# Gated attention and feed-forward decode on one core: sixteen small loads behind the second item's keys

## The chip, the cores and the metric

The kernel runs on one core of a Trainium2 chip. The metric is the time of one execution on the device in microseconds. TensorE is called PE here, VectorE DVE, ScalarE ACT, GpSimd POOL and SyncE SP; SP issues every DMA of this kernel, and 16 DMA engines carry them out.

## The reference

Two tokens (batch B = 2, one position each, width D = 640) go through attention with 32 heads over a cache of 4096 keys and values of 128 numbers per head, and through a feed-forward layer of width 1728. A gate mixes the two results. All is float32.

```python
def reference(A_x, A_k_cache, A_v_cache, A_wq, A_wo, B_x, B_w1, B_w2, gate_w):
    x = A_x
    g = sigmoid((x * gate_w).sum(-1, keepdims=True))
    q = (x @ A_wq).reshape(B, 1, 32, 128).transpose(0, 2, 1, 3)
    p = softmax(einsum("bhqd,bhkd->bhqk", q, A_k_cache) * 128 ** -0.5)
    o = einsum("bhqk,bhkd->bhqd", p, A_v_cache)
    a = o.transpose(0, 2, 1, 3).reshape(B, 1, 4096) @ A_wo
    b = einsum("bsf,fd->bsd", silu(einsum("bsd,df->bsf", x, B_w1)), B_w2)
    return g * a + (1 - g) * b
```

The keys and the values are 134 MB each; wq and wo are 10.5 MB each, w1 and w2 4.4 MB each.

## The kernel before

The attention is cut into 16 items: eight groups of four heads, times two batches. An item has one load of keys and one of values, each 128 partitions of 64 KB (8.4 MB). SBUF holds three such slabs: "v" for values, "a" and "b" for the keys of even and odd items. Since "a" and "b" alternate, the keys of item i + 2 can be loaded when the scores of item i are made, and the values of item i + 1 when PE has used those of item i.

Per item, POOL and DVE multiply the keys by the query, each a part of the slab (lines 670 and 676); DVE sums the products into scores (line 686) and finds the peak (lines 694 to 704); ACT makes the exponentials (line 715); PE multiplies them by the values (line 766); DVE and PE then bring the result into the columns of `oP` (lines 788 to 837). Before the items stand the query weights wq (line 608) and the feed-forward layer: w1 is loaded into slab "a", DVE forms the hidden row (lines 443 and 446), spreads and turns it into the buffer `turned` (line 499), and ACT and DVE make `seq` from it (lines 500 to 512). Nothing reads `turned` after line 512. After the items, PE multiplies `oP` by wo (lines 556 and 586), and one store of 5 KB writes the output.

The order on each engine is the order in which the program writes its operations. A small planner (`Flow.plan`, line 75) goes through all operations and gives each one the waits on semaphores that its reads and writes need, and leaves out those that are already implied. `Flow.dma` (line 67) records a DMA; all of them are on SP, so they have line 69 in the profile. SP works through its list in order: an instruction that waits holds up all that stand behind it. A DMA has a semaphore of its own unless one is given by `signal`, which it raises by 16 when all of it has landed.

SP's list around the change: w1, x, gate, w2, wq, a store of zeros, then the keys of the first item (`load_k(0)`, line 470), the values of the first item and the keys of the second (`load_v(0)` and `load_k(1)`, lines 656 and 657), and then, from the loop at line 853, `load_k(i + 2)` and `load_v(i)` in turn. In the texts below k0, k1, k2 are the keys of the first, second and third item, and v0 the values of the first.

Of the kernel before, what the change touches and what calls it, by code (L numbers as in the profile page):

```python
# [158 lines left out]
def gated_decode(nc, x, kc, vc, wq, wo, w1, w2, gate, out):  # L159
# [31 lines left out]
    f = Flow(nc)  # L191
    V, S_, T_, G_ = nc.vector, nc.scalar, nc.tensor, nc.gpsimd

    def sb(name, shape, align=32):
        return nc.alloc_sbuf_tensor(name, shape, F32, align_bytes=align)[tuple([slice(None)] * len(shape))]
# [9 lines left out]
    def part(n, *ks):  # L205
        return [f"{n}.{k}" for k in (ks or range(8))]
# [21 lines left out]
    turned = sb("turned", [P, FR * 32])  # L228
# [17 lines left out]
    oT = ps_m[:64, 256:512].rearrange("p (n r) -> p n r", r=32)  # L246
    early, acc = ps_acc[:, :W2], ps_0[:, :W]

    h_q, h_e, h_v, h_o = (f.sem(n) for n in ("next_q", "weights", "values", "rows"))


# [9 lines left out]
    def kslab(i):  # L261
        return "a" if i % 2 == 0 else "b"
# [4 lines left out]
    def run_of(flat, i):  # L267
        hq, b = items[i]
        return flat[b, hq].rearrange("(p c) -> p c", p=P)

    def load_k(i):
        n = kslab(i)
        f.dma("SP", slab[n], run_of(kflat, i), writes=part(n))
# [3 lines left out]
    def load_v(i):  # L277
        src = run_of(vflat, i)
        if i < N - 1:
            v_load[i] = f.dma("SP", slab["v"], src, writes=part("v"), signal=h_v if i < LOOPED else None)  # L280
            return
        f.dma("SP", slab["a"], src, writes=part("a"))
# [112 lines left out]
    for e in range(2):  # L395
        ends, at = join[:, e, ::HB], 64 + HB * (1 - e)
# [40 lines left out]
    for b in range(B):  # L437
        for j in range(J):
            at = xt[:, j, HB * b : HB * b + 1]
# [177 lines left out]
    def mm_query(i):  # L617
        return T_.matmul(  # L618
            ps_q[:, :DH],
            spread,  # L620
            qall.rearrange("p h b d -> p (h b) d")[:, i, :],
            start=True,
            stop=True,
        )

    def query(i, by=(), loop=None):
        u, b = items[i][0] // HALF, items[i][1]
        fn = (lambda: mm_query(i)) if loop is None else (lambda it: mm_query(it + i))
        f.op(
            "PE",  # L630
            fn,
            reads=["spread", f"qall{u}{b}"],
            writes=["ps_q"],
            by=by,
            loop=loop,
            lower=[(h_q, 1)],
        )

    def copy_q(i):
        f.op("ACT", lambda: S_.copy(qsb, ps_q[:, :DH]), reads=["ps_q"], writes=["qsb"])  # L640
# [14 lines left out]

    load_v(0)
    load_k(1)
    query(0)
    copy_q(0)

# [4 lines left out]
    def products(i):  # L665
        k = slab[kslab(i)].rearrange("p (c d) -> p c d", d=DH)
        k0, k1 = part(kslab(i), 0), part(kslab(i), 1)
        f.op(
            "POOL",
            lambda: G_.tensor_mul(k[:, CV:, :], k[:, CV:, :], qsb[:, None, :].to_broadcast([P, C - CV, DH])),  # L670
            reads=["qsb"] + k1,
            writes=k1,
        )
        f.op(
            "DVE",
            lambda: V.tensor_mul(k[:, :CV, :], k[:, :CV, :], ps_q[:, None, :DH].to_broadcast([P, CV, DH])),  # L676
            reads=["ps_q"] + k0,
            writes=k0,
        )

    def scores(i):
        k = slab[kslab(i)].rearrange("p (c d) -> p c d", d=DH)
        for n, (c0, c1) in enumerate(((0, CV), (CV, C))):
            ops["scores", i] = f.op(
                "DVE",
                lambda c0=c0, c1=c1: V.reduce_sum(Ss[i % 2][:, c0:c1], k[:, c0:c1, :], axis=AX.X),  # L686
                reads=part(kslab(i), n),
                writes=[f"s{i % 2}{n}"],
            )

    def peak(i):
        t = ps_m
        s = Ss[i % 2]
        f.op("DVE", lambda: V.reduce_max(t[:, :1], s, axis=AX.X), reads=[f"s{i % 2}0", f"s{i % 2}1"], writes=["m0"])
        f.op(
            "DVE",
            lambda: V.tensor_scalar_mul(t[:, 32:64], t[:, :1].to_broadcast([P, 32]), -SCALE),
            reads=["m0"],
            writes=["m1"],
        )  # L700
        f.op("DVE", lambda: V.transpose(t[:, 64:96], t[:, 32:64]), reads=["m1"], writes=["m2"])
        f.op(
            "DVE",
            lambda: V.tensor_reduce(nb, t[:, 64:96], axis=AX.X, op=ALU.min),
            reads=["m2"],
            writes=["nb"],
        )

    def weights(i):
        s = Ss[i % 2]  # L710

        def fn():
            for q in range(Q):
                lo, hi = q * QP, (q + 1) * QP
                last = S_.activation(  # L715
                    pz[lo:hi, :, 4 * q : 4 * q + 4],
                    s[lo:hi].rearrange("p (g c) -> p g c", c=4),
                    AF.Exp,
                    bias=nb[lo:hi],
                    scale=SCALE,  # L720
                    accum_out=rs[lo:hi],
                )
            return last

        ops["exp", i] = f.op(
            "ACT",
            fn,
            reads=["nb", f"s{i % 2}0", f"s{i % 2}1"],
            writes=["pz", "rs"],
            signal=h_e if i < LOOPED else None,  # L730
        )

    def relay(i):
        ops["relay", i] = f.op("ACT", lambda: S_.sem_inc(h_q), after=[ops["scores", i]], signal=None)
        ops["relay", i].signal = "sent"

    def total(i, by=(), loop=None):
        f.op(
            "PE",
            lambda *_: T_.matmul(  # L740
                ps_t[:, :1], fold.rearrange("p a q c -> p (a q c)"), rs, start=True, stop=True
            ),
            reads=["fold", "rs"],
            writes=["ps_t"],
            by=by,
            loop=loop,
            lower=[(h_e, 1)],
        )

    def invert(i):  # L750
        b = items[i][1]
        f.op("DVE", lambda: V.reciprocal(ps_t[:, 1:2], ps_t[:, :1]), reads=["ps_t"], writes=["ps_t1"])
        f.op(
            "DVE",
            lambda: V.tensor_scalar(rg, ps_t[:, 1:2], g[:, b : b + 1], None, op0=ALU.mult),
            reads=["ps_t", "ps_t1", "g"],
            writes=["rg"],
        )

    def values(i, by=(), loop=None):  # L760
        v = slab["v" if i < N - 1 else "a"].rearrange("p (g c) -> p g c", g=NG)

        def groups(*_):
            for gr in range(NG):
                q = gr % 4
                last = T_.matmul(  # L766
                    ps_v[32 * q : 32 * q + 32, :],
                    pz[:, gr, :],
                    v[:, gr, :],
                    start=(gr < 4),  # L770
                    stop=(gr >= NG - 4),
                )
            return last

        f.op(
            "PE",
            groups,
            reads=part("v" if i < N - 1 else "a") + ["pz"],
            writes=["ps_v"],
            by=by,  # L780
            loop=loop,
            lower=[(h_v, 16)],
        )
# [69 lines left out]
    for i in range(N + 1):  # L853
        j = i - 1
        loop = j if 0 <= j < LOOPED else None

        def by(what):
            return [ops[what, i if what == "relay" else j]] if loop is not None else ()

        if i < N:  # L860
            products(i)
        if j >= 0:
            total(j, by=by("exp"), loop=loop)
            values(j, by=[v_load[j]] if loop is not None else (), loop=loop)
            invert(j)
        if 1 <= i < N:
            load_v(i)
        if i < N:
            scores(i)
            if i < LOOPED:  # L870
                relay(i)
            if i + 2 < N:
                load_k(i + 2)
            peak(i)
            weights(i)
        if i == N - 1:
            v_users = f.users(part("v"))
            for g_ in range(NP):
                load_wo(g_)
        if j >= 0:  # L880
            combine(j)
            gather(j, by=by("combine"), loop=loop)
            turn(j)
        if i + 1 < N:
            query(i + 1, by=[ops["relay", i]], loop=i)
            copy_q(i + 1)
# [28 lines left out]
    for e, (a, b) in spans.items():  # L915
        ops, at = f.ops[e], 0
        while at < len(ops):
            end = at
            if at == a:
                f.once(e, ops[a:b])  # L920
                at = b
            elif ops[at].loop is None:
# [3 lines left out]
                at = end  # L926
            else:
# [3 lines left out]
                at = end  # L931
# [21 lines left out]
```

## Time and profile before

| | |
|---|---|
| median of 3 runs | 695.9 us (695.77 to 696.06) |
| profiled execution, first to last instruction (span) | 694.2 us |
| profiled execution, other time | none is given |
| instructions | 3593 |
| read from HBM | 298.26 MB |
| mean rate over the span | 430 GB/s |
| granted PE clock, mean of the span | 0.666 |

The times are those of the device for one execution. The span belongs to one further execution, taken by the profiler. In the profile's page, busy times are per engine; the line of slices cuts the span into 40 equal parts and gives the busy share of each in tenths; the queue lines give packets, MB and the time of the packets as a share of 16 DMA engines' time. In the timeline of SP, a row has the start, the duration, the operation and the tensor it writes and reads. In the table by stage, each engine has its busy time and count, and the last three columns are the granted PE clock, the share of the DMA engines' time and GB/s. In a view of the DMA over a chosen window, the same 40 slices cut that window, and each packet's bytes stand in the slice where it starts.

### The profile page before, as it was taken

Reading aid. Unit: us, or ns where it says so; the run is one execution under the profiler, and the core shown is the slowest. Engines: PE = TensorE matmul, PEld = TensorE weight load, DVE = VectorE, ACT = ScalarE, POOL = GpSimd, SP = SyncE. Lnnn points to the kernel's source line nnn. Section 1 sums busy time; section 2 is a strip of 40 time slices with the busy share of each in tenths; the row PEclk is TensorE's granted clock in tenths of the full one; section 3 lists DMA queues with packets and bytes.
Section 4 is the critical chain, followed back from the end, with each engine's and each line's share of the span. In section 5 each row is a group of like instructions: output and inputs, shape, how many; then the busy total and the mean of one; then the engine's idle time right before and its main releaser. Section 6 shows DMA issues by size and latency. Waiting matters only on the chain. (4 is left out here: it accounts for less than half of the span.)

```text
span 694.2 us, 3593 instructions
## 1 busy us (share of the span) xinstructions
PE 211.4 (30%) x1440; PEld 72.5 (10%) x1440; DVE 507.5 (73%) x269; ACT 40.0 (6%) x152; POOL 265.6 (38%) x26
## 2 busy tenths in 40 slices
PE   0074032151331405060412306060503315050657
PEld 0032010010110101020100101010100101010113
DVE  3810958898989596886959596986959595977811
ACT  0001010101010101010010101010000101010000
POOL 1000808191726090815335180906244270907100
PEclk9998556565565757575665757575655757575689
DMA  9999999999999999999999999999999999999997
GB/s 383 430 446 450 430 427 424 423 457 438 427 430 423 430 461 427 434 423 423 438 457 427 430 423 427 464 430 430 423 423 461 434 430 427 423 438 457 427 408 326
DMA packets 6209, 298.33 MB, mean 430 GB/s; under 512 B 672, under 2 KB 700, under 8 KB 956
## 3 DMA queue, kind: packets, MB, share of 16 engines
q1 hardware_dynamic: 6204, 298.27, 99.4%
q8 instruction: 2, 0.03, 0.0%
q14 instruction: 3, 0.02, 0.0%
HBM read 298.26 MB, written 0.01 MB: 430 GB/s over the span
## 5 line engine op out<-in xcount | busy, mean ns | idle before, releaser
L670 POOL TENSOR_TENSOR slabs<-slabs,qsb 128x7680 f32<-128x7680 f32 x16 | 262.3, 16396 | 378.7 <-DMA slabs<-in_A_k_cache_dram 347.8
L686 DVE TENSOR_REDUCE s<-slabs 128x68 f32<-128x8704 f32 (+1 forms) x32 | 276.3, 8676 | 0.0
L766 PE MATMUL ps<-slabs,pz 128*32 128x512 f32 x1024 | 146.2, 735 | 345.2 <-PEq L145 338.2
L676 DVE TENSOR_TENSOR slabs<-slabs,ps 128x8704 f32<-128x8704 f32 x16 | 147.5, 9218 | 108.5 <-DMA slabs<-in_A_k_cache_dram 108.4
L766 PEld LDWEIGHTS ps<-slabs,pz 128*32 128x32 f32 x1024 | 39.5, 132 | 438.6 <-issue 431.6
L715 ACT ACTIVATE pz<-s,nb 32x128 f32<-32x128 f32 x64 | 25.4, 398 | 556.5 <-PE ps L766 363.2
L804 PE MATMUL ps<-osb,pick 128*128 128x512 f32 x32 | 20.4, 724 | 58.9 <-PEq L145 58.0
L818 DVE TENSOR_REDUCE row<-ps 64x128 f32<-64x512 f32 x16 | 10.9, 682 | 23.3 <-PE ps L804 23.3
L788 DVE SCALAR_TENSOR_TENSOR osb<-ps,rg,own 128x512 f32<-128x512 f32 x16 | 12.0, 748 | 21.4 <-PE ps L766 21.2
L618 PE MATMUL ps<-qall,spread 128*128 (+1 forms) x32 | 7.4, 319 | 35.3 <-PEq L145 34.5
L446 DVE SCALAR_TENSOR_TENSOR slabs<-slabs 128x1728 f32<-128x1728 f32 x8 | 16.1, 2019 | 0.3
L458 PE MATMUL ps<-slabs,xz_col 128*32 128x432 f32 x16 | 3.1, 928 | 33.2 <-DVE slabs L446 33.2
L804 PEld LDWEIGHTS ps<-osb,pick 128*128 128x128 f32 x32 | 5.4, 211 | 73.0 <-issue 71.2
L715 ACT ACTIVATION_READ_ACCUMULATOR pz<-s,nb 32x1 f32 x64 | 11.8, 184 | 0.0
L618 PEld LDWEIGHTS ps<-qall,spread 128*128 128x128 f32 x32 | 6.9, 224 | 44.9 <-issue 43.2
L533 PE MATMUL ps<-slabs,seq 128*32 128x320 f32 x54 | 10.3, 545 | 3.7 <-DVE seq L512 3.7
L825 DVE STREAM_TRANSPOSE ps<-row 64x256 f32<-64x256 f32 x16 | 10.3, 642 | 0.6
L608 PE MATMUL ps<-slabs,xz_col 128*32 128x512 f32 x80 | 9.8, 593 | 0.0
L891 DVE COPY slabs<-ps 128x160 f32<-128x160 f32 x1 | 0.3, 325 | 12.2 <-PE ps L586 12.2
L556 PE MATMUL ps<-slabs,oP_xs 128*32 128x320 f32 x96 | 8.8, 433 | 1.4 <-DMA slabs<-in_A_wo_dram 1.4
L740 PE MATMUL ps<-rs,fold 128*128 128x1 f32 x32 | 6.1, 260 | 2.3 <-PEq L145 2.1
L740 PEld LDWEIGHTS ps<-rs,fold 128*128 128x128 f32 x32 | 5.7, 222 | 5.0 <-issue 3.5
(63 smaller groups left out, 71.9 us busy)
## 6 DMA issues: line engine op xcount, KB each, us to landing
slabs<-in_A_wq_dram SPq DMA_DIRECT2D x1, 10240.0 KB, 44.5
slabs<-in_B_w_dram SPq DMA_DIRECT2D x2, 4320.0 KB, 17.0
slabs<-in_A_wo_dram SPq DMA_DIRECT2D x1, 5120.0 KB, 21.5
slabs<-in_A_wo_dram SPq DMA_DIRECT2D x2, 1280.0 KB, 25.4
slabs<-in_A_wo_dram SPq DMA_DIRECT2D x1, 1600.0 KB, 30.1
slabs<-in_A_wo_dram SPq DMA_DIRECT2D x1, 640.0 KB, 31.1
slabs<-in_A_wo_dram SPq DMA_DIRECT2D x1, 320.0 KB, 31.4
slabs<-in_A_k_cache_dram SPq DMA_DIRECT2D x16, 47.8
```

The lines of the kernel that those rows point to most:

```text
L446: lambda b=b, j=j, at=at: V.scalar_tensor_tensor(hsum[:, b, :], w1t[:, j, :], at, hsum[:, b, :], op0=ALU.mult, op1=ALU.add)
L533: last = T_.matmul(early[to : to + 32, :], seq[:, k : k + 2, :].rearrange("p k z -> p (k z)"), slab[n][:, k * HD : (k + 1) * HD], start=(k ...
L618: return T_.matmul(ps_q[:, :DH], spread, qall.rearrange("p h b d -> p (h b) d")[:, i, :], start=True, stop=True,)
L670: lambda: G_.tensor_mul(k[:, CV:, :], k[:, CV:, :], qsb[:, None, :].to_broadcast([P, C - CV, DH])),
L676: lambda: V.tensor_mul(k[:, :CV, :], k[:, :CV, :], ps_q[:, None, :DH].to_broadcast([P, CV, DH])),
L686: lambda c0=c0, c1=c1: V.reduce_sum(Ss[i % 2][:, c0:c1], k[:, c0:c1, :], axis=AX.X),
L715: last = S_.activation(pz[lo:hi, :, 4 * q : 4 * q + 4], s[lo:hi].rearrange("p (g c) -> p g c", c=4), AF.Exp, bias=nb[lo:hi], scale=SCALE, ...
L740: lambda *_: T_.matmul(ps_t[:, :1], fold.rearrange("p a q c -> p (a q c)"), rs, start=True, stop=True),
L766: last = T_.matmul(ps_v[32 * q : 32 * q + 32, :], pz[:, gr, :], v[:, gr, :], start=(gr < 4), stop=(gr >= NG - 4),)
L788: lambda: V.scalar_tensor_tensor(osb, ps_v.rearrange("p (c d) -> p c d", d=DH), rg, own[:, :, None].to_broadcast([P, 4, DH]), op0=ALU.mult ...
L804: lambda *_: T_.matmul(ps_o, pick, osb.rearrange("p c d -> p (c d)"), start=True, stop=True),
L818: lambda: V.reduce_sum(row, ps_o[:64].rearrange("p (c d) -> p d c", d=DH), axis=AX.X),
```

## The change

Behind `load_k(1)`, sixteen loads from w1 go into `turned`: the n-th one takes n rows of 16 + n numbers (68 to 128 bytes a row), at columns that lie side by side. They share one semaphore, `cells`. Behind the load of keys in round 3 of the loop, SP waits until this semaphore stands at 256, that is until all sixteen have landed. Nothing reads what they bring.

```diff
+    h_cell = f.sem("cells")
     h_q, h_e, h_v, h_o = (f.sem(n) for n in ("next_q", "weights", "values", "rows"))
...
     load_v(0)
     load_k(1)
+    for n in range(1, 17):
+        at = sum(16 + m for m in range(1, n))
+        to = turned[:n, at : at + 16 + n]
+        f.dma("SP", to, w1[:n, : 16 + n], signal=h_cell, after=f.users(["turned"]))
     query(0)
     copy_q(0)
...
                 load_k(i + 2)
             peak(i)
             weights(i)
+        if i == 3:
+            f.op("SP", lambda: nc.sync.wait_ge(h_cell, 256)).signal = "sent"
```

On SP, right behind the values of the first item and the keys of the second, the rows now read as follows; `turned` is the buffer, `in_B_w_dram` is w1, and 1x17 means one row of 17 numbers.

```order
 L69 DMA slabs<-in_A_v_cache_dram 128x16384 [waits done_PE]
 L69 DMA slabs<-in_A_k_cache_dram 128x16384
+L69 DMA turned<-in_B_w_dram 1x17
+L69 DMA turned<-in_B_w_dram 2x18
+L69 DMA turned<-in_B_w_dram 3x19
+L69 DMA turned<-in_B_w_dram 4x20
```

Before, the keys of the third item stood here; none of the new rows waits for anything. The end of the piece, still on SP, is this:

```order
+L69 DMA turned<-in_B_w_dram 14x30
+L69 DMA turned<-in_B_w_dram 15x31
+L69 DMA turned<-in_B_w_dram 16x32
 L69 DMA slabs<-in_A_k_cache_dram 128x16384 [waits done_DVE]
 L69 DMA slabs<-in_A_v_cache_dram 128x16384 [waits done_PE]
```

The keys of the third item, with their wait for DVE, have moved back by sixteen rows. The wait for `cells` shows on SP further down, at the load that follows it, the fifth item's values:

```order
 L69 DMA slabs<-in_A_v_cache_dram 128x16384 [waits done_PE]
 L69 DMA slabs<-in_A_k_cache_dram 128x16384 [waits done_DVE]
-L69 DMA slabs<-in_A_v_cache_dram 128x16384 [waits done_PE]
+L69 DMA slabs<-in_A_v_cache_dram 128x16384 [waits done_PE,cells]
 L69 DMA slabs<-in_A_k_cache_dram 128x16384 [waits done_DVE]
```

The load has kept its wait for PE and stands behind that for `cells` as well. On PE, DVE, ACT and POOL the order is the same as before.

## The prediction

> **What bounds the kernel now.** I read the page first: busy shares, the DMA line of the 40 slices, and the queues.
>
> ```profile
> PE 211.4 (30%) x1440; PEld 72.5 (10%) x1440; DVE 507.5 (73%) x269; ACT 40.0 (6%) x152; POOL 265.6 (38%) x26
> DMA  9999999999999999999999999999999999999997
> DMA packets 6209, 298.33 MB, mean 430 GB/s; under 512 B 672, under 2 KB 700, under 8 KB 956
> q1 hardware_dynamic: 6204, 298.27, 99.4%
> ```
>
> No compute engine is busy for more than 73% of the span; the 16 DMA engines are busy for 99.4% of it, and all of that is one queue, the one that SyncE (SP) feeds. The table by stage says whether that average hides a stage with another limit.
>
> ```profile
> 48.00:106.00 58.00, 20.63 (x154) 9.06 (x154) 27.42 (x7) 4.80 (x14) 16.39 (x1) 0.65 1.00 433
> 106.00:300.00 194.00, 50.36 (x310) 17.21 (x302) 169.18 (x75) 11.12 (x45) 98.47 (x6) 0.60 1.00 433
> 300.00:660.00 360.00, 107.29 (x697) 34.04 (x697) 280.80 (x133) 21.98 (x89) 147.48 (x9) 0.64 1.00 434
> ```
>
> The last two columns are the DMA share and GB/s: 1.00 and 433 to 434 in each stage from 48 to 660 us. So the queue never runs dry there, and the rate is the same whether DVE works 27.42 of 58 us (47%) or 169.18 of 194 (87%). The end is set by the same queue, as the chain that ended last shows:
>
> ```profile
> 659.21 30.07 DMA slabs<-in_A_wo_dram
> 689.42 2.19 PE ps L586 x56
> 692.15 0.33 DVE slabs L891
> ```
>
> The last weights come in behind everything else, then follow 2.2 us of matmuls, one copy and the store. The rule for this kernel is therefore simple: time put on the slowest of the 16 DMA engines lengthens the run one for one; time put on SP, or on a DMA engine that is ahead of the slowest, costs nothing until the queue runs empty.
>
> **The change, part by part.** It removes nothing. It adds sixteen load instructions on SP between the load of the second item's keys (k1) and of the third item's (k2), 136 short rows with their semaphore writes on the DMA engines, and one wait on SP behind the load of the sixth item's keys (k5).
>
> *SP's time.* What a small load costs SP is in its own timeline; the second, third and last of these rows are the x, gate and zero-output transfers of 4 or 8 short rows.
>
> ```profile
> 0.74 0.38 SPq L69 DMA_DIRECT2D slabs<-in_B_w_dram  x1
> 1.85 0.73 SPq L69 DMA_DIRECT2D oP_xs<-in_A_x_dram  x1
> 2.63 0.56 SPq L69 DMA_DIRECT2D oP_xs<-in_gate_w_dram  x1
> 3.23 0.43 SPq L69 DMA_DIRECT2D slabs<-in_B_w_dram  x1
> 4.18 0.59 SPq L69 DMA_DIRECT2D out_dram<-oP_xs  x1
> ...
> 59.51 0.33 SPq L69 DMA_DIRECT2D slabs<-in_A_v_cache_dram  x1
> 59.88 0.44 SPq L69 DMA_DIRECT2D slabs<-in_A_k_cache_dram  x1
> 94.92 0.33 SPq L69 DMA_DIRECT2D slabs<-in_A_k_cache_dram  x1
> 108.34 0.33 SPq L69 DMA_DIRECT2D slabs<-in_A_v_cache_dram  x1
> ...
> 657.80 2.79 SPq L69 DMA_DIRECT2D slabs<-in_A_wo_dram  x6
> ```
>
> The small ones take 0.73, 0.56 and 0.59 us, mean 0.63, and 0.04 us lie between neighbours (2.63 + 0.56 = 3.19, next at 3.23). Sixteen take 16 x 0.67 = 10.7 us, from 60.32 to about 71.0. The next instruction in line is the load of k2 at 94.92, which waits for DVE:
>
> ```profile
> SPq L69 <- DVE ps L694: 75.4, 4, 34.9
> 106.97 9.22 DVE L676 TENSOR_TENSOR slabs<-slabs,ps 128x8704 f32<-128x8704 f32 x1 [11.02 <-DMA slabs<-in_A_k_cache_dram]
> ```
>
> The longest of these waits is the 34.9 us between 60.0 and 94.9, so the 10.7 us lie inside it with 23.9 to spare, and I cost them at 0. Without that cover k2 would go out 10.7 us late, and a second reserve would take most of that: k1, which DVE gets at 106.97, keeps the queue busy until about 106, 11 us behind 94.9. The new loads bring no wait of their own, since what reads their buffer is done before the values' load ahead of them goes out.
>
> *The DMA engines' time.* 136 rows of 68 to 128 bytes are 14.7 KB, or 0.03 us at 430 GB/s; it is the packets that count. A stretch that holds nothing but small ones is the final store (the last three lines; the first two are from the page's list of DMA issues):
>
> ```profile
> slabs<-in_A_k_cache_dram SPq DMA_DIRECT2D x16, 47.8
> slabs<-in_A_v_cache_dram SPq DMA_DIRECT2D x16, 29.4
> ...
> DMA  0004000045400045500010500000100000000000
> DMA packets 12, 0.01 MB, mean 26 GB/s; under 512 B 4, under 2 KB 12, under 8 KB 12
> q1 hardware_dynamic: 12, 0.01, 9.9%
> ```
>
> This is 693.7 to 693.9 us: eight rows of 640 bytes and four semaphore writes take 9.9% of 16 engines x 0.2 us = 0.32 us, 26 ns a packet. How are the new packets spread? The page counts 672 packets under 512 bytes. With 41 large loads (32 of keys and values, six of the output weights, w1, w2 and wq) of 16 semaphore writes each (656), the other 16 are four each for the four small transfers, whose row count is 4 on one side. So a load of 4 rows ran on four engines, and I take it that one of n rows runs on n. The engine that all sixteen use then gets 16 rows and 16 semaphore writes, 32 x 26 ns = **0.84 us**, and the one that only the last uses gets 0.05 us. The bounds for the time at the end are 0 (if the slowest engine is one with few) and 0.84 us (if it is the one with all); were all rows put on one engine it would be 136 + 16 = 152 packets, 4.0 us, which the count of four speaks against. The Trainium skill, "DMA: Bandwidth & Descriptors", section on why a DMA increments its semaphore by 16, says the same of the spread: the largest number up to 16 that divides both row counts, on the lowest-numbered engines. By that, engine 0 takes 16 loads and engine 15 one; the 672 agrees with the number, and no row here shows the numbering.
>
> Who is slowest? The 16 engines finish each load one after another; this is the landing of the last keys, 646.3 to 647.7 us, in slices of 35 ns:
>
> ```profile
> DMA  0099099999990090090000000009000000099000
> GB/s 0 0 1873 1873 0 1873 1873 5618 1873 1873 1873 1872 0 0 1872 0 0 1873 0 0 0 0 0 0 0 0 0 1872 0 0 0 0 0 0 0 1872 1873 0 0 0
> ```
>
> Each 1873 is one engine that starts its next load. Thirteen are through by slice 17, then come single ones in slices 27, 35 and 36. The last is 19 slices, 0.67 us, behind the thirteenth. So an engine among the thirteen must gain over 0.67 us before the end notices; at most 0.84 - 0.67 = 0.17 us gets through there. Only if one of the last three carries many of the loads does more of it show. I take **+0.2 us**, nearer to 0 than to 0.84: rows of 68 to 128 bytes should not take longer than rows of 640, thirteen engines in sixteen are covered down to 0.17 us, and of n engines on average only half the loads reach one.
>
> *The wait.* It stands behind these rows' first and ahead of their second:
>
> ```profile
> 198.67 0.33 SPq L69 DMA_DIRECT2D slabs<-in_A_k_cache_dram  x1
> 231.98 0.33 SPq L69 DMA_DIRECT2D slabs<-in_A_v_cache_dram  x1
> ```
>
> Queued behind it are the fifth item's values and all later loads. The small loads follow k1 on the queue and land soon after 107 us, 90 us before SP gets there, and the next load waits for PE until 231.98 anyhow. Cost 0.
>
> *Sum.* 0 + 0.2 + 0: the span goes from 694.2 to 694.4 us. The page gives the profiled execution's span and no other time of it; the median of the three runs, 695.9, is 1.7 us above it, which stays. **696.1 us.**
>
> **Rivals.**
>
> 1. *SP is held up by too many open transfers.* When the small loads go out, the first keys (k0), the first values (v0) and k1 are open, so with the last small one 19 may be. The most that the trace shows to be open at once is 7: at 657.80 six loads go out in 2.79 us, with no stall, while the last values are still arriving. If 7 is the limit, four small loads go out at 60 us, one more as k0 and one as v0 lands, and the other ten when k1 has: 10 x 0.67 = 6.7 us, then k2's own issue of 0.4 and the time to its first packet, under the 1.3 us of the lone store in rival 2. The engines stand empty for some 8 us, which a queue at 100% never gets back: 694.2 + 8 + 1.7 = **704 us**, slower. It decides only if the limit is below 18 (k1, sixteen small ones and k2 itself at 94.9). For it: nothing in the trace goes beyond 7. Against it: those seven are large loads with far more rows than these, and they went out without a pause. 7%.
>
> 2. *Each small load holds its engine for a round trip.* The final store is alone on the queue:
>
> ```profile
> 692.50 0.58 SPq L69 DMA_DIRECT2D out_dram<-slabs  x1
> ```
>
> It is issued at 692.50, and its last packet stands in slice 28 of the 5 ns slices shown above, 693.84: 1.3 us. Sixteen in a row on one engine would be 21 us: 694.2 + 21 + 1.7 = **717 us**; with only part of it exposed, at least 698. Against it stands the place where x and gate pass between two weight loads:
>
> ```profile
> DMA  0009099900190990219190900000000090090000
> DMA packets 52, 0.56 MB, mean 561 GB/s; under 512 B 24, under 2 KB 36, under 8 KB 36
> ...
> DMA  0009909990090990009909900000000009090000
> ```
>
> The first line is 12.6 to 13.6 us, where 12 rows of x and gate go through, the other 22.8 to 23.8 us, one load later. The first engine is in slice 3 both times and the last in 36 and 35: no engine fell back by 1.3 us, let alone by two. What is not shown is sixteen in a row. The Trainium skill speaks for this rival in the same page: under "Anatomy of one DMA" a transfer costs about 2.0 us beyond its bytes, and its "Rules for kernel authors" would have small transfers merged. An estimate by that page, if the 2.0 us held the engine, is 16 x 2.0 = 32 us; the same section says that most of it is the wait for the completion, which occupies nobody here, and the two lines above agree. 6%.
>
> 3. *It gets faster,* by a shift of the engines' order against each other: the queue has nothing to give up but the 0.6% that is not busy, and the change takes no byte away. 694 us, 2%.
>
> **How the numbers follow.** The forecast has 85%. A measurement of this kernel tells about 0.2%, 1.4 us, from no change, and the forecast's whole span of 0 to 0.84 us lies inside that. The range for 8 in 10 is the forecast's own: below, 695.5 (the runs before reach down to 695.77, and an engine that shifts may give 0.2); above, 695.9 + 0.84 and 0.4 for the runs' own spread, 697.1. It leaves out the 13% of the first two rivals and half of the third. Faster 2%, same 85%, slower 13%.
>
> **What would show it.** In the profile after, sixteen rows for the small loads at 60.3 to 71 us of about 0.6 us each on SP, and k2 at 94.9 as now; a gap among them, or k2 after 106, is rival 1. The packets should be 6209 + 136 + 136 = 6481, 944 of them under 512 bytes; other counts mean another spread. The DMA share from 48 to 660 us should still be 1.00. The landing of k2 should show an engine at most 0.84 us further back than now; a step of over 1 us there is rival 2. SP should wait for the new semaphore for no time that can be seen. I would be wrong if one engine takes several hundred ns for each small load, since all sixteen meet on it.

## The result and the profile after

| | before | with the change |
|---|---|---|
| median | 695.93 us (8 runs) | 698.2 us (8 runs, 697.85 to 698.39) |
| ratio, 95% interval | | 1.0031 (1.0021 to 1.0041) |
| span of the profiled execution | 694.2 us | 695.8 us |
| time of the profiled execution | not given | 698.32 us |

The kernel is 2.3 us slower, outside the range that was given. The span of the profiled execution grew by 1.6 us, but a single span is a poor measure: the 694.2 us of before is the shortest that was seen. The record has the span of the other executions too. The eight with the change have spans of 695.5 to 696.0 us (median 695.8), and each takes about 2.4 us more than its span. Of the kernel before, 91 executions ran beside the experiments below. Their spans are 694.2 to 695.4 us (median 694.5); 82 of them take 1.3 to 1.7 us more than their span (median of all 1.4), and nine take 2.1 to 2.7 us more. So some 1.3 us of the loss lie in the span and some 1.0 us outside it. These two parts turned out to have different causes. One execution, among the eleven of the run with thirty-two idle instructions, took 1250.31 us; it is left out of that run's ratio, and nothing here explains it.

The page of the changed kernel counts its packets:

```profile
DMA packets 6481, 298.35 MB, mean 429 GB/s; under 512 B 944, under 2 KB 972, under 8 KB 1228
```

Packets and small packets are as many as forecast, 6481 and 944. The queue is busy for 99.2% of the span (99.4% before). SP's timeline around the small loads:

```profile
59.46 5.67 SPq L69 DMA_DIRECT2D turned<-in_B_w_dram  x16
95.33 0.35 SPq L69 DMA_DIRECT2D slabs<-in_A_k_cache_dram  x1
```

All sixteen go out in 5.7 us without a pause, and the third item's keys (k2) follow at 95.3 as before: SP is not held up. The table by stage (its last two columns are the DMA share and GB/s) shows where the rate falls:

```profile
48.00:106.00 58.00, 19.32 (x152) 8.65 (x152) 27.42 (x7) 4.80 (x14) 16.39 (x1) 0.65 1.01 432
106.00:300.00 194.00, 51.09 (x302) 17.34 (x294) 167.76 (x74) 11.12 (x45) 98.43 (x6) 0.60 1.00 431
300.00:660.00 360.00, 105.74 (x694) 33.69 (x694) 282.13 (x133) 20.61 (x84) 147.49 (x9) 0.64 1.00 434
```

After 300 us it is 434 GB/s again; the loss is in the stages around 106 us, where the small loads pass, while the engines' share still reads 1.00. So packets are under way all the time, but they take longer for their bytes. The chain that ended last is the same as before, about 1.5 us later (690.93 in place of 689.42 for the last matmuls):

```profile
690.93 2.22 PE ps L587 x56
```

Before, k2's first packets all took the same time. This is the queue's line for 105 to 107 us, where the first packet of k2 starts on each of the 16 engines, next to 16 semaphore writes of 9 ns:

```profile
q1 hardware_dynamic: 32, 1.05, 121.3%
```

1.213 x 16 engines x 2 us = 38.8 us; less 0.1 us for the semaphore writes, that is 2.42 us a packet. What happens with the change shows in the view of the DMA over windows so narrow that a single 64 KB packet starts in them. The share is that of 16 engines over the window, so share x 16 x window is the packet's duration. The windows are 106.953 to 106.957, 105.372 to 105.375, 106.244 to 106.247 and 105.746 to 105.747 us; each holds k2's first packet on one engine, behind 4, 8, 11 and 16 small loads on that engine:

```profile
q1 hardware_dynamic: 1, 0.07, 3778.1%
...
q1 hardware_dynamic: 1, 0.07, 5962.5%
...
q1 hardware_dynamic: 1, 0.07, 7825.0%
...
q1 hardware_dynamic: 1, 0.07, 27387.5%
```

That is 37.781 x 16 x 0.004 = 2.42 us behind four loads, and 2.86, 3.76 and 4.38 us behind eight, eleven and sixteen. The change is its own series of doses, since its loads put 1 to 16 of them on the engines. Each engine can be followed through the trace, because a packet starts where the one ahead of it ends. The first packet behind n small loads takes

| loads ahead | 1 to 4 | 5 | 6 | 7 | 8 | 9 | 10 | 11 | 12 | 13 | 14 | 15 | 16 |
|---|---|---|---|---|---|---|---|---|---|---|---|---|---|
| us over 2.42 | 0 | 0.02 | 0.14 | 0.27 | 0.44 | 1.03 | 1.17 | 1.34 | 1.38 | 1.46 | 1.70 | 1.74 | 1.96 |

The rows themselves take 12 to 13 ns each and a load with its semaphore write some 15 ns, as little as one could hope. The price stands in the large packet behind them. Followed on to the last keys, the engine that finishes them last is the one with eleven loads, at 649.1 us; it had reached k2 later than 14 of the others. Before, the last engine finishes these keys at 647.6 us. These 1.5 us are what the span shows.

### The profile page after: what moved, and what is told of

Its sections match the earlier page's. It is cut to its first block, busy times and chain, and to the rows that moved or that the text cites. A ratio compares the mean times of both kernels' runs of the same rounds, so it can differ in the third digit from the quotient of the medians.

```text
span 695.8 us, 3610 instructions
## 1 busy us (share of the span) xinstructions
PE 210.3 (30%) x1440; PEld 72.4 (10%) x1440; DVE 507.6 (73%) x269; ACT 40.0 (6%) x152; POOL 265.5 (38%) x26
## 2 busy tenths in 40 slices
DMA packets 6481, 298.35 MB, mean 429 GB/s; under 512 B 944, under 2 KB 972, under 8 KB 1228
## 3 DMA queue, kind: packets, MB, share of 16 engines
q1 hardware_dynamic: 6476, 298.29, 99.2%
## 5 line engine op out<-in xcount | busy, mean ns | idle before, releaser
L830 DVE STREAM_TRANSPOSE ps<-row 64x256 f32<-64x256 f32 x16 | 10.3, 642 | 0.6
```

The lines of the kernel that those rows point to most:

```text
L830: lambda: V.transpose(oT.rearrange("p n (e i) -> p n e i", e=2), twice),
```

## The experiments

Two theories were stated first. Theory 1: a DMA engine prepares loads some way ahead of what it is writing, which is called its lead here, and a run of more than about five small loads uses this lead up, so that the next large packet waits. Theory 2: each small load costs its engine about 0.14 us wherever it stands. For the time outside the span, the question was whether the loads or the longer program of SP cause it.

The lines with + stand in place of the loop with the sixteen loads, or beside it where the text says so; the lines around them are not shown. SP's wait in round 3 stays, and waits for as much as each version adds to the semaphore. A span is that of the profiled execution; medians are given beside those of the kernel before that ran with them, with the ratio and its 95% interval.

**Groups of four.**

```diff
+    def small(k):
+        for n in range(4 * k + 1, 4 * k + 5):
+            at = sum(16 + m for m in range(1, n))
+            to = turned[:n, at : at + 16 + n]
+            f.dma("SP", to, w1[:n, : 16 + n], signal=h_cell, after=f.users(["turned"]))
+    small(0)
...
                 load_k(i + 2)
+            if i < 3:
+                small(i + 1)
```

> The same sixteen small loads, but in four groups of four, behind the keys of the second, third, fourth and fifth item. In the trace of the change, the 64 KB packet behind a run of small loads on one DMA engine takes 2.42 us after 1 to 4 loads, 2.44 after 5, 2.86 after 8, 3.45 after 9 and 4.38 after 16. Theory 1 (a run of more than about five small loads uses up a lead that the engine's reads have, and the next large packet then waits): no group is longer than four, so no large packet behind them is over 2.5 us, and only the rows' own 0.015 us each remain: span 694.2 to 694.6. Theory 2 (each small load costs its engine about 0.14 us wherever it stands): 695.5 to 695.9 as with the change. The time outside the span stays at 2.4 us if it comes from the longer program.

Span 694.6 us, median 697.15 beside 695.82 (ratio 1.0016, 1.0007 to 1.0025). No first packet behind a group is over 2.6 us in the trace. The queue's line for 105 to 107 us is nearly that of before, and the stage from 106 to 300 us is back at 433 GB/s:

```profile
q1 hardware_dynamic: 52, 1.05, 122.0%
...
106.00:300.00 194.00, 50.69 (x314) 17.23 (x302) 168.79 (x75) 11.12 (x45) 98.48 (x6) 0.60 1.00 433
```

The same 136 rows, semaphore writes and instructions lose their price in the span when no run is longer than four: theory 2 falls. The time outside the span stayed: 2.7 us in the profiled execution, 2.4 in the median of the eleven.

**Sixteen equal loads.**

```diff
+    for n in range(16):
+        f.dma("SP", turned[:16, 28 * n : 28 * n + 28], w1[:16, :28], signal=h_cell, after=f.users(["turned"]))
```

> Sixteen loads of 16 rows each (28 numbers a row) in place of 1 to 16 rows, so that each of the 16 DMA engines gets all sixteen. Theory 1: every engine has what only the first one has in the change, 16 rows of 0.015 us and a next packet of 4.38 instead of 2.42 us; all landings of the next keys move back by 2.2 us, the spread between the engines stays near that of before, and the span is 694.2 + 2.2 = 696.4. If the stretch were a matter of the low-numbered engines or of how unequal the engines' loads are, the span would be under 695.5.

Span 696.6 us, median 699.09 beside 695.82 (1.0042, 1.0028 to 1.0055). In the window 105 to 107 us all 16 first packets of k2 start, with 528 small ones:

```profile
q1 hardware_dynamic: 544, 1.08, 245.5%
```

2.455 x 16 engines x 2 us = 78.6 us; less 5.8 us for the small packets (256 of 13 ns, 272 of 9) that is 4.55 us for each large one. All engines wait alike, so it is neither low numbers nor unequal shares.

**One load with as many rows.**

```diff
+    f.dma("SP",
+        turned[:, :64].rearrange("p (a c) -> p a c", a=2)[:, :, :28],
+        w1[:P, :64].rearrange("p (a c) -> p a c", a=2)[:, :, :28],
+        signal=h_cell, after=f.users(["turned"]))
...
-            f.op("SP", lambda: nc.sync.wait_ge(h_cell, 256)).signal = "sent"
+            f.op("SP", lambda: nc.sync.wait_ge(h_cell, 16)).signal = "sent"
```

> One load of 128 partitions with two pieces of 28 numbers each instead of the sixteen: 16 rows on each engine as in the run with sixteen equal loads, but one semaphore write on each instead of sixteen. If the lead is used up by rows, the next large packet is 4.3 us on every engine and the span 696.4; if by packets of any kind (17, as with eight loads of a row and a semaphore write), about 2.9 us and 694.8; if by loads, each closed by its semaphore write, 2.42 us and 694.3.

Span 694.6 us, median 696.31 beside 695.82 (1.0005, 0.9996 to 1.0014: no difference). In the same window, 105 to 107 us, 15 first packets of k2 start, with 288 small ones:

```profile
q1 hardware_dynamic: 303, 1.01, 124.6%
```

39.9 us less 3.6 for the small packets, over 15 large ones: 2.42 us. Sixteen rows on an engine cost nothing if they come as one load. What delays the next packet is the loads, each with its semaphore write, and not the rows.

**Eight loads of two rows per engine**, to hold loads against packets:

```diff
+    for n in range(8):
+        f.dma("SP", turned[:32, 28 * n : 28 * n + 28], w1[:32, :28], signal=h_cell, after=f.users(["turned"]))
```

> Eight loads of 32 rows of 28 numbers: each DMA engine gets two rows and one semaphore write from each, 24 packets in all. In the traces so far the packet behind eight loads is longer by 0.44 to 0.47 us and behind nine by 1.01 to 1.03, a step of over 0.5 where the others are 0.1 to 0.25. If loads count, the packets behind are 2.9 us (eight loads) and the span is 694.2 + 0.7 = 694.9. If packets count (24 packets are those of twelve loads of one row), they are 3.8 us, with the step, and the span is 695.8.

Span 695.2 us, median 696.75 beside 696.28 (1.0007, 0.9998 to 1.0016). The window 105 to 107 us again:

```profile
q1 hardware_dynamic: 416, 1.08, 163.8%
```

This is 52.4 us; less 4.6 for the small packets, each large one took 2.99 us. That is the number for eight loads (2.9), not that for 24 packets (3.8). The profiled span lies between the two forecasts, but these started from 694.2. The median span of the ten executions, 695.15, is 0.65 above the 694.5 of before, and the forecast for loads was 0.7.

**Twenty-four loads**, to see whether the loss ends:

```diff
+    for n in range(24):
+        f.dma("SP", turned[:16, 16 * n : 16 * n + 16], w1[:16, :16], signal=h_cell, after=f.users(["turned"]))
```

> Twenty-four loads of 16 rows of 16 numbers. From sixteen equal loads (next packets of 4.3 to 4.9 us, mean 4.56) on, eight more at 0.14 us each make 5.7 us, and the span 696.6 + 8 x 0.155 = 697.8. If the step seen between eight and nine comes again between sixteen and seventeen, 6.2 us and 698.3. If the lead of the reads were all that is lost, once, the packets stay at 4.6 us and the span at 696.7.

Span 698.1 us, median 701.3 beside 696.28 (1.0071, 1.0056 to 1.0086). In the window 105 to 107.6 us, which holds the sixteen first packets of k2 and 784 small ones, the queue has a share of 254.1%. 2.541 x 16 x 2.6 us = 105.7 us; less 10.3 for the small packets, that is 6.0 us for each large one. The loss goes on with each load, at about (6.0 - 4.55) / 8 = 0.18 us, and is no single lead that is lost once. The profiled execution is the fastest of the four. The other three have spans of 699.1 to 699.3, above both forecasts, and no profile was taken of these. So whether a second step stands between sixteen and seventeen can't be read from this.

**Sixteen loads of one row.**

```diff
+    for n in range(16):
+        f.dma("SP", turned[:1, 28 * n : 28 * n + 28], w1[:1, :28], signal=h_cell, after=f.users(["turned"]))
```

> Sixteen loads of one row of 28 numbers each: all on one DMA engine, which is then the only one with a longer packet. Theory 1: that packet takes 4.4 us, its engine falls back by 2.2 us, and the end moves only by what this engine is then behind the engine that was last before. In the trace of the change the engine with sixteen loads finished the keys before them 0.46 us after the first engine, and the last one at the end stood 1.2 us after the first: 0.46 + 2.2 - 1.2 = 1.5, span 695.2 to 695.8. If the end followed the sum over all engines (16 packets instead of 136 rows), it would be under 694.5.

Span 695.1 us, median 697.51 beside 695.88 (1.0022, 1.0013 to 1.0031). One engine has a longer packet, alone in the window 105.690 to 105.692:

```profile
q1 hardware_dynamic: 1, 0.07, 13325.0%
```

133.25 x 16 x 0.002 = 4.26 us. This one engine of 16 moves the end of the profiled execution by 0.9 us (by 0.6 in the median span of all executions). That is less than the 2.1 us that it lost with its rows, because it stood ahead of the slowest engine before. It now finishes the last keys last, at 648.5 us, where the last one of before had 647.6. The end follows the slowest engine, as the forecast had it; the forecast was 0.1 us too high.

**Rows of 432 numbers.**

```diff
+    for n in range(16):
+        to = (turned, spaced.rearrange("p n r -> p (n r)"))[n // 8]
+        p0 = 16 * (n % 8)
+        f.dma("SP", to[p0 : p0 + 16, :432], w1[p0 : p0 + 16, :432], signal=h_cell, after=f.users(["turned", "spaced0", "spaced1"]))
```

> Sixteen loads of 16 rows as in the run of sixteen equal loads, but with 432 numbers a row instead of 28, spread over two dead buffers. The rows take 16 x 0.084 = 1.3 us on each engine instead of 0.25. If each load takes a fixed time of about 0.15 us on the reading side of an engine, and the writing side only shows what of it its own rows do not cover, the next packet is stretched by about 1.0 us instead of 2.1, and the span stays at 696.6. If the stretch is a fixed latency behind many loads, the next packet stays at 4.5 us and the span is 697.7.

Span 698.0 us, median 700.01 beside 695.88 (1.0062, 1.0048 to 1.0076). Neither forecast held. The packets behind take 3.3 to 3.8 us, less than the 4.55 behind narrow rows, as the first forecast had it. But the rows themselves are stretched too: 97 of the 256 take 0.072 us, the rest more, up to 0.30, and the mean is 0.105 (the forecast's 0.084 was an estimate). The span is near that of the second forecast, with a median of 697.6 us. So it seems that the waiting is not only in the packet behind the last load, and that wider rows take up part of it themselves.

**Copies from SBUF.**

```diff
-        f.dma("SP", to, w1[:n, : 16 + n], signal=h_cell, after=f.users(["turned"]))
+        f.dma("SP", to, spaced.rearrange("p n r -> p (n r)")[:n, : 16 + n], signal=h_cell, after=f.users(["turned", "spaced0", "spaced1"]))
```

> The sixteen loads of the change with 1 to 16 rows, but copied from another dead buffer in SBUF instead of from w1 in HBM. If the time per load is that of a read from HBM, the packets behind them are near 2.42 us and the span is 694.2 to 694.6; if it is the engine's own handling of a load, they are as long as with the change, up to 4.4 us, and the span is 695.8.

Span 696.1 us, median 698.17 beside 695.88 (1.0032, 1.0020 to 1.0044). The same window has almost the same share as with the change, whose line comes first here:

```profile
q1 hardware_dynamic: 304, 1.06, 170.1%
```

```profile
q1 hardware_dynamic: 304, 1.06, 170.9%
```

The trace has the same series, 0.47 us behind eight loads, 1.01 behind nine, 1.92 behind sixteen. So it is not a read from HBM that is waited for. Of the two causes in the forecast, the engine's own handling of the loads is left.

**No loads, and sixteen, eight or thirty-two other instructions on SP**, for the time outside the span. Each only raises the semaphore by one; they are called idle here, since they move nothing:

```diff
+    for n in range(16):
+        f.op("SP", lambda: nc.sync.sem_inc(h_cell)).signal = "sent"
```

(the wait for 16; in the other two runs 8 and 32 in place of 16)

> No small load at all; sixteen increments of the semaphore on SP in their place, and the same wait in round 3, so that SP's program has as many instructions as with the change. Both theories: span 694.2. The time outside the span, 1.7 us before and 2.4 with the change, stays 2.4 (696.6 in all) if it comes from SP's longer program, and is 1.7 (695.9) if it comes from the loads.

> No small loads; eight increments of the semaphore on SP and the wait, half as many instructions as in the run with sixteen. Span 694.2. If the time outside the span grows with each SP instruction, it is 2.0 us, half-way between 1.7 and 2.4; if it comes from one more fetch of instructions beyond a certain length, it is either 1.7 (695.8) or 2.4 and more (696.7 to 697.1).

> No small loads; thirty-two increments on SP and the wait. Span 694.3. The time outside the span was 1.5 us with eight increments and 2.4 in the profiled run with sixteen (median 697.1 against 695.8 us). If it is one more fetch of instructions past a length between the two, the median stays at 696.7 to 697.3; if it grows with each instruction, it is over 698.

Sixteen: span 694.3, median 697.11 beside 695.82 (1.0019, 1.0010 to 1.0028). Eight: 694.3, median 695.81 beside 695.88. Thirty-two: 694.5, median 695.83 beside 696.28 (0.9994, 0.9985 to 1.0003). So sixteen idle instructions cost 1.3 us with nothing changed in the span, and neither eight nor thirty-two cost anything that can be measured. All eleven executions with sixteen take 2.4 us or more beyond their span, and all with eight or thirty-two 1.3 to 1.5. It is no price per instruction, and not one for every program past a length either, as both forecasts for thirty-two had assumed. What differs is a fetch of instructions. The view of the DMA over 694.5 to 699.5 us (slices of 0.125 us), first for the change, then for sixteen instructions:

```profile
DMA  0000001000000000000000020000000000000000
q14 instruction: 1, 0.01, 0.5%
```

```profile
DMA  0000000000020000000000000000000000000000
q14 instruction: 1, 0.01, 0.6%
```

A fetch of 8 KB starts at 697.4 and 695.9 us, 1.6 us after the span's last instruction. With eight instructions there is none in that window. With thirty-two it stands in the window 665.5 to 665.7 us, well inside the span:

```profile
q14 instruction: 1, 0.01, 9.7%
```

The same holds in all fourteen profiled executions whose time is known: in the nine with a fetch behind the span's end the execution takes 2.1 to 2.7 us more than its span, in the five without one 1.3 to 1.5 us. In one of the nine, that of the single load, it is a fetch of 16 KB on another queue, q8.

**Both causes taken away in turn.** Sixteen more increments ahead of the sixteen loads, which should move the fetch into the span; then the same ahead of the groups of four. The loads stay as they were:

```diff
+    for n in range(16):
+        f.op("SP", lambda: nc.sync.sem_inc(h_cell)).signal = "sent"
...
-            f.op("SP", lambda: nc.sync.wait_ge(h_cell, 256)).signal = "sent"
+            f.op("SP", lambda: nc.sync.wait_ge(h_cell, 272)).signal = "sent"
```

> The change with its sixteen loads in a row, and sixteen more increments on SP ahead of them, 33 added instructions in all. If the time outside the span comes from a fetch of instructions that falls behind the span's end, this fetch stands inside the span here (near 665 us, under other waits), the span is 695.6 to 696.1 as with the change, the time outside 1.3 to 1.7, and the median 697.2 to 697.5. If the loads themselves cause it, the median stays at 698.2.

> The sixteen loads in four groups of four and the same sixteen increments. With both causes gone, the long packets and the late fetch, the span is 694.2 to 694.7 and the median 695.7 to 696.2, not to be told from before. If the loads cost anything else, it is over 696.5.

The change with more instructions: span 695.6, median 697.14 beside 695.86 (1.0020, 1.0011 to 1.0029); the fetch is at 665.0 us, the profiled execution took 697.10, 1.5 more than its span. All eleven executions of it stay 1.3 to 1.7 us above their spans, where all eight of the change stand about 2.4 above theirs. In groups, with more instructions: median 696.27 beside 695.86 (1.0000, 0.9991 to 1.0009). Its profiled execution was its slowest (696.69, span 695.2, also 1.5 apart), and its median span, 694.9, is above the forecast of 694.2 to 694.7, too. Sixteen instructions more made the change about 1 us faster. With the runs of loads broken up as well, no difference from before can be measured; the interval leaves room for some 0.6 us. No version was measurably faster than the kernel before.

## Why the prediction was wrong

- **What bounds the kernel: right.** The DMA queue sets the time, and the end followed the slowest engine where it was followed through the trace, with the change, with equal loads and with loads of one row.
- **SP's time at 0: right**, with 5.7 us in place of 10.7; a small load costs SP 0.35 us, not 0.67. The first rival, a limit on open transfers, did not appear with up to nineteen open.
- **The spread over the engines: right.** 6481 packets, and doses of 1 to 16 loads on the engines.
- **The step that failed is the bound of 0.84 us** ("32 x 26 ns"). It priced small packets by their own durations in the final store, and took that as what they cost the engine. Their own time was even shorter, 0.24 us for sixteen, but behind more than four or five loads in a row the next packet waits, by up to 1.96 us. So the busiest engine loses 2.2 us, not 0.84. The end moved back by 1.3 to 1.6 us in place of the forecast's 0.2. The reasoning on which engine is late was right in kind: the engine with sixteen loads stood ahead and gave up part of its loss, and one of the late engines, with eleven loads, carried the end. With 2.2 in place of 0.84, the sum's upper bound for the span would have been 696.4, and 695.8 lies below it.
- **The second rival was close in kind, not in size.** I put 1.3 us on each load, if it held its engine for a round trip, and argued from x and gate that nothing is held. But those are two loads in a row, and up to four cost nothing. By the sign that the prediction gave for it, a step of over 1 us at k2, this rival came true; by its price of 21 us it did not. The runs show 0.14 to 0.18 us for each load past the fourth or fifth, with a step between eight and nine. The 2.0 us per transfer in the Trainium skill, "DMA: Bandwidth & Descriptors", section "Anatomy of one DMA", are given there for transfers that GpSimd issues, and SP issues all of them here. An estimate by them was 32 us; behind sixteen loads of the change, 1.96 us stood in the way of the next packet.
- **The wait at 0: right.** SP waited 34.1 us there, until 233.5, and what ended this was PE, not the semaphore.
- **"1.7 us above, which stays": wrong**, and the second term that was mis-sized. It set the median of three executions against the span of a fourth, the shortest; the time outside the span was 1.4 us before and is 2.4 with the change. The longer program of SP goes with a fetch of instructions behind the span's end. Moving this fetch into the span with sixteen more instructions gave the 1.0 us back. Alone, this term would have left the result in the range: 694.4 + 2.4 = 696.8 us. The one above would not: 695.8 + 1.7 = 697.5 us, where the range ends at 697.1.

What is shown: the loss comes with loads in a row on one engine, from HBM or from SBUF, and not with the number of short rows. What is only argued: that an engine prepares each load in some 0.14 us ahead of its writes, hidden while a 64 KB packet is being written and exposed when the writes take 15 ns. The same page of the Trainium skill, "Two DMAs through the same engine are not ordered", says that an engine's reading and writing sides are separate queues, which fits; no run here sees the two apart. Open are the step between eight and nine loads, and whether the load itself or its semaphore write takes the time: each load had one, and all of a version's loads raised the same semaphore.

For the time outside the span, the fetch goes with the loss in every profiled execution, and moving it moved the loss. That the wait for the fetch is what takes the time is argued. One program can also do both: of the eleven executions of the single load, eight take 1.3 to 1.5 us beyond their span and three, the profiled one among them, 2.4 to 2.5, like nine of the 91 of before. What decides between them was not found.

## What to carry to other kernels

On a DMA queue that is always full, the cost of small transfers is to be looked for in the packet behind them, and a price taken from two in a row does not hold for sixteen: here four in a row between large loads cost nothing beyond their own 15 ns each, and sixteen cost their engine 2.2 us. Many rows as one load, or few loads at a time, avoid it. A difference under 0.2% between two programs can also come from nothing but the length of an engine's program; the time of each execution beside its own span, and a control with idle instructions, tell that apart.

## What was not expected of the hardware

- One load of 16 rows per DMA engine left the next 64 KB packet at 2.42 us; sixteen loads of one row per engine made it 4.55, and twenty-four about 6 us, with the source in HBM or, for the change's loads, in SBUF alike.
- From eight to nine small loads ahead, the added time goes from 0.44 to 1.03 us (0.47 to 1.01 with the source in SBUF), while the other neighbours differ by 0.02 to 0.24.
- Sixteen idle instructions on SP made the execution 1.3 us longer (by the medians) at the same span, and eight or thirty-two did not. The Trainium skill, "Runtime: NRT & Kernel Launch", section "Instruction fetch mechanics", calls the fetch of the next block mostly hidden; that holds here for the fetch at 665 us, and not for the one behind the span's end.
